# A second place for exponentials, and weight loads on ACT's DMA queue, in an attention kernel with a feed-forward part

## The chip, the cores and the metric

The kernel runs on one core of a Trainium2 chip. The core's engines work side by side, each through its own list of instructions in order: PE (TensorE: matmuls and transpositions, with PEld for loading its stationary operand), DVE (VectorE), ACT (ScalarE), POOL (GpSimd), and SP (SyncE), which here issues DMAs. Engines wait for each other by semaphores. Data lies in HBM, in SBUF (128 partitions) or in PSUM, where PE writes. The metric is the time of one execution in microseconds (us) on the device; less is better.

## What is computed

Softmax attention over 8 batches x 8 heads x 576 rows of width 64, in which each row keeps only the scores within tau of its maximum, and then a feed-forward layer on the 4608 tokens (512 wide, 2048 hidden, softplus between):

```python
scores = scale * np.matmul(q, k.transpose(0, 1, 3, 2))
thresh = np.max(scores, axis=-1, keepdims=True) - tau
scores = np.where(scores >= thresh, scores, -1000000000.0)
scores = scores - np.max(scores, axis=-1, keepdims=True)
attn = np.exp(scores)
attn = attn / (np.sum(attn, axis=-1, keepdims=True) + 1e-09)
attn_out = np.matmul(attn, v).astype(np.float32)
x = np.ascontiguousarray(attn_out.transpose(0, 2, 1, 3)).reshape(B * S, H * D)
h = x @ w_in
g = np.maximum(h, 0.0) + np.log1p(np.exp(-np.abs(h)))
return (g @ w_out).astype(np.float32)
```

`w_in` and `w_out` come as 64-bit floats; the kernel reads them as pairs of 32-bit words and makes 32-bit floats of them on the chip.

## The kernel before

**Attention.** A unit is one pair of heads of one batch: 32 units, nine tiles each, 288 tiles in all. A tile is 128 query rows against 576 keys. Tiles 0 to 3 belong to the unit's first head, tiles 5 to 8 to its second, and tile 4 (`NC`) holds the last 64 rows of both. `mate` makes pairs of tiles 0 and 1, 2 and 3, 5 and 6, 7 and 8; tile 4 is alone.

For each tile, PE makes the scores in one of two PSUM banks (`scores`, L423). DVE takes the row's maximum and a threshold (`row_max`, L430 and L431). ACT takes the exponentials of all scores into SBUF, into one half of `e_all` (`exps`, L435). DVE multiplies them by "score at or above threshold" in place and sums them (`mask`, L440). PE transposes the result (`weights_T`, L474, four blocks of 128 columns; L471 and L477 for the last 64), ACT copies it out (`weights_hi`, L498 to L515), and PE multiplies it with the values (`values`; in the first units by `slow_products`, L549, three matmuls per tile).

`e_all` has two halves of 576 columns. Tiles use them by turns (`half`, the parity of the tile's number in the whole order). The two tiles of a pair lie so that their last 64 columns are neighbours; for the second tile of a pair, L471 transposes 128 columns that run across the border of the halves, for both tiles at once.

In the first five units (`NF`, attribute `whole`, 45 tiles) the weights stay in one 32-bit part and the products are fp32. From the sixth unit on they are split in a high and a low part, and the low part goes to buffers of tag `gL` (two of them). For the first 36 tiles (`TG`) the transposed weights go to PSUM banks of their own; later they go to the bank of the tile's scores.

**Feed-forward.** The tokens go in chunks of 512. For each chunk, x is read back from HBM (`load_x`, L613), split in two parts (`split_x`: L127 on ACT, L132 on POOL), multiplied with `w_in` (`hidden`, L645 to L649), put through softplus (L667) and multiplied with `w_out` (`project`, L703 to L707). The first chunk may start at tile 41. Before it, x of the fourth unit has to be scaled and stored: row scales to HBM (L583), back as `R` (L587), the product on POOL (L593), x out (L597), x in (L613).

**Weights.** There are 32 blocks of 128 x 512 (16 of `w_in`, 16 of `w_out`). `to_f32` loads a block's words (L185, 512 KB), and some steps later ACT takes an absolute value of the high words (L193), POOL clamps it (L194), DVE assembles the bits in three instructions (`second`: L200, L202, L205), and POOL splits the result (L125, L132). `w_in` goes back to HBM in this form (L234) and is read from there in every chunk (L629). `took` is the number of spare buffers that a block got; with two it takes them from the 16 that will hold `w_out`. Block n is begun at tile 2n. `later_(WD, first)` puts the first use four points behind the load; a tile has two points.

**Order.** The program text lists a tile's steps by the letters of `PAT0` (first 36 tiles) or `PAT`. A scheduler then orders the instructions of each engine by its own estimate of times; `behind(i, others)` adds a constraint that instruction i stands after the last of `others` and adds no wait. All DMAs of the kernel before are issued by SP in order; a DMA whose buffer is not free holds those behind it. Every DMA also takes one of eight completion semaphores in turn, and waits until the transfer that used that semaphore before it is complete, wherever that one was issued.

Of the kernel before, what the change touches and what calls it, by code (L numbers as in the profile page):

```python
# [9 lines left out]
F32 = mybir.dt.float32  # L10
F32R = mybir.dt.float32r
U32 = mybir.dt.uint32
AF = mybir.ActivationFunctionType
# [10 lines left out]
P = 128  # L24
# [35 lines left out]
def tile_kernel(ctx: ExitStack, tc: tile.TileContext, q, k, v, tau, w_in, w_out, out):  # L60
# [8 lines left out]
    nc = tc.nc  # L69
    B, H, S, D = q.shape  # L70
    NT, DM = out.shape
    DFF = w_in.shape[1]
    SM = 512
    SR = S - SM
    HS = S // 2
# [60 lines left out]
    free, held = [NFC], [0]  # L136

    masked = []
    scored = []

    def behind(i, others):

        if others:
            tc.add_manual_dep(i.ins, others[-1].ins.name, mybir.DependencyInfo(
                mybir.DependencyClass.NoSync, mybir.DependencyReason.DATA), reason="order")
# [4 lines left out]
    def to_f32(src, want, name, then):  # L150

        keep = 1 if want else 0
        while free[0] < 1 + keep and free[0] < NFC - held[0]:
            force()
        took = max(0, min(2, free[0] - keep))
        if took:
            words = piece(F32R, f"wc_{name}")
        else:  # L160
            words = wpool.tile([P, 2, DM], F32R, tag="wi", bufs=WB, name=f"wc_{name}")
        if took > 1:
            m = piece(F32, f"wa_{name}")[:, 0, :]
        else:
            m = fpool.tile([P, 512], F32, tag="st", bufs=NST, name=f"ws_{name}")
        free[0] -= took + keep
        held[0] += keep

        later_ = defer if took > 1 else lambda n, f: f()
        step = 2 if held[0] < NFC // 2 else 1  # L170
        w = piece(F32R, f"wo_{name}") if want else words

        def done():
            free[0] += took

        def parts():
            hi_of(nc.gpsimd, w[:, 0, :], m)
            lo_of(nc.gpsimd, w[:, 1, :], m, w[:, 0, :])

        if src.dtype == F32:  # L180
            nc.sync.dma_start(m, src)
            later_(WD, lambda: then(parts, w, done))
            return
        words = words.bitcast(U32).rearrange("p a n -> p (a n)")
        nc.sync.dma_start(words, src.bitcast(U32))  # L185
        words = words.rearrange("p (n t) -> p n t", t=2)
        low, high = words[:, :, 0], words[:, :, 1]
        mu = m.bitcast(U32)

        def first():
            nc.scalar.activation(m, high.bitcast(F32), AF.Abs, scale=2.0 ** 16)  # L193
            nc.gpsimd.tensor_scalar(out=m, in0=m, scalar1=W_MAX, scalar2=W_MIN, op0=ALU.min, op1=ALU.max)  # L194
            later_(1, lambda: second(0))


        def second(n):
            if n == 0:
                i = nc.vector.tensor_scalar(out=mu, in0=mu, scalar1=3, scalar2=None, op0=ALU.logical_shift_left)  # L200
            elif n == 1:
                i = nc.vector.scalar_tensor_tensor(out=mu, in0=high, scalar=0x80000000, in1=mu,  # L202
                                                   op0=ALU.bitwise_and, op1=ALU.bitwise_or)
            else:
                i = nc.vector.scalar_tensor_tensor(out=mu, in0=low, scalar=29, in1=mu,  # L205
                                                   op0=ALU.logical_shift_right, op1=ALU.bitwise_or)
            if took > 1:
                behind(i, masked)
            if n < 2:
                later_(step, lambda: second(n + 1))  # L210
            else:
                later_(1, lambda: then(parts, w, done))

        later_(WD, first)
# [184 lines left out]

    e_all = cpool.tile([P, 2, S], F32, name="e_all")
    banks = [ps_s.tile([P, 2, 512], F32, tag="s", name=f"s_{i}") for i in range(SB)]
    nth = [0]

    def scores(s, t):
        if t == s.tiles[0]:
            s.sums = apool.tile([P, 9], F32, tag="sums", name=f"sums_{s.i}")
            s.half, s.sp, s.m, s.grp = {}, {}, {}, {}
        sp = banks[nth[0] % SB]  # L410
        s.half[t] = half = nth[0] % 2
        nth[0] += 1
        s.sp[t] = sp
        if t == NC:
            parts = [(qm[:, n, j, :], j) for j in range(2) for n in range(2)]
        else:
            j = 0 if t < NC else 1
            c = t if t < NC else t - NC - 1
            parts = [(s.qT[j][n][:, c * P:(c + 1) * P], j) for n in range(2)]
        k0 = (1 - half) * SR  # L420
        for m, (lhs, j) in enumerate(parts):
            for hf in range(2):
                i = nc.tensor.matmul(sp[:, hf, 0:HS], lhs, s.kT[j][:, k0 + hf * HS:k0 + (hf + 1) * HS],  # L423
                                     start=(m == 0), stop=(m == len(parts) - 1))
        scored.append(i)
# [6 lines left out]
        s.m[t] = (negm, thr)  # L432

    def exps(s, t):
        nc.scalar.activation(e_all[:, s.half[t], :].rearrange("p (h n) -> p h n", h=2), s.sp[t][:, :, 0:HS],  # L435
                             AF.Exp, bias=s.m[t][0], scale=1.0)

    def mask(s, t):
        e2 = e_all[:, s.half[t], :].rearrange("p (h n) -> p h n", h=2)
        masked.append(nc.vector.scalar_tensor_tensor(  # L440
            out=e2, in0=s.sp[t][:, :, 0:HS], scalar=s.m.pop(t)[1], in1=e2, op0=ALU.is_ge, op1=ALU.mult,
            accum_out=s.sums[:, s.tiles.index(t):s.tiles.index(t) + 1]))
# [8 lines left out]
    def mate(s, t):  # L451

        if t == NC:
            return None, False
        u = t if t < NC else t - 1
        return (t + 1, False) if u % 2 == 0 else (t - 1, True)

    def weights_T(s, t):
        half = s.half[t]
        e = e_all[:, half, :]  # L460
        other, second = mate(s, t)
        lone = other is None
        if 9 * NPAIR * s.b + 9 * s.hp + t < TG:
            main = ps_g.tile([P, NC, P], F32, tag="g", name=f"tm_{s.i}_{t}")
            rest = ps_g.tile([P, NC, P], F32, tag="g", name=f"tr_{s.i}_{t}")[:, 0, :] if lone or second else None
        else:
            sp = s.sp[t]
            main = sp[:, 0, :].rearrange("p (c n) -> p c n", n=P)
            rest = sp[:, 1, 0:P]
        if second:  # L470
            nc.tensor.transpose(rest, e_all.rearrange("p h n -> p (h n)")[:, SM:SM + P], ident)  # L471
        for c in range(NC):
            c0 = half * SR + c * P
            nc.tensor.matmul(main[:, c, :], e[:, c0:c0 + P], ident, is_transpose=True, start=True, stop=True)  # L474
        if lone:
            r0 = 0 if half else SM
            nc.tensor.transpose(rest[0:SR, :], e[:, r0:r0 + SR], ident)  # L477
        s.sp[t] = (main, rest)
# [520 lines left out]
```

## Time and profile before

| what | us |
|---|---|
| time, median of 3 runs (lowest to highest) | 1449.85 (1448.56 to 1451.9) |
| the profiled execution | 1451.43 |
| its span from first to last instruction | 1449.6 |
| PE in the chain of work that ended last | 78% of the span |
| DVE, ACT, DMA and POOL in that chain | 8%, 4%, 3%, 3% |

The profile is of one execution. "Busy" is the time in which an engine had an instruction in work. For an engine that works in order, the idle time ahead of an instruction is put down to what released it last. A row "A <- B: 6.7, 9, 1.7" says that A's engine sat idle ahead of A until B ended, 6.7 us in total, in 9 cases, at most 1.7 us. A row of the timeline gives start, duration, engine, line, operation, and out <- in; in square brackets stands the idle time ahead of it with its releaser. SPq is SP's sequencer, which issues DMAs.

### The profile page before, as it was taken

The page shows a single profiled execution, that of the slowest core. Times are in us where ns is not written, and L with a number is a line of the kernel's source. Part 1 is how long each engine was busy: PE and PEld are TensorE (multiplying, and loading weights), DVE is VectorE, ACT ScalarE, POOL GpSimd, SP SyncE. Part 2 cuts the span into 40 slices and gives each one's busy share as a digit, 9 for nine tenths or more (in the row PEclk, how much of TensorE's full clock was granted, in tenths as well). Part 3 has the DMA queues.
Part 4 walks back from the last instruction along what each step waited for, and adds up shares of the span by engine and source line. Part 5 has one row for each costly group of instructions (what it writes and reads, how often), then busy time and mean ns, then how long its engine had stood idle before and what let it go on. Part 6 is the DMA issues. An engine that isn't in the chain of part 4 may idle for free.

```text
span 1449.6 us, 23487 instructions
## 1 busy us (share of the span) xinstructions
PE 1398.8 (96%) x7860; PEld 1161.8 (80%) x7860; DVE 987.2 (68%) x2211; ACT 847.1 (58%) x1615; POOL 590.3 (41%) x619
## 2 busy tenths in 40 slices
PE   6887999999999999999999999999999999999998
PEld 4555688788888888888888888888888888788886
DVE  6988588787777777777777777777777777402111
ACT  6667667667656576657665665667665765311010
POOL 3667566443333333344334333344334431324221
PEclk9999999999999999999999999999999999999999
DMA  5866765445333533445433533354344432333321
GB/s 170 227 186 206 214 191 182 126 121 160 104 106 114 135 109 116 119 132 151 122 111 96 154 105 100 117 151 120 113 119 135 147 99 73 105 126 130 118 86 44
DMA packets 131208, 189.93 MB, mean 131 GB/s; under 512 B 35312, under 2 KB 86800, under 8 KB 131088
## 3 DMA queue, kind: packets, MB, share of 16 engines
q1 hardware_dynamic: 131088, 188.43, 44.5%
q8 instruction: 63, 1.03, 0.3%
q14 instruction: 57, 0.47, 0.1%
HBM read 140.51 MB, written 27.41 MB: 116 GB/s over the span
## 4 chain that ended last, share of the span: by engine, by line
PE 78%; DVE 8%; ACT 4%; issue 3%; DMA 3%; POOL 3%; SPq 1%; POOLq 0%; DVEq 0%; ACTq 0%
PE s L423 10%; PE h L647 9%; PE h L645 9%; PE h L649 8%; PE o L707 8%; PE o L705 8%; PE o L703 8%; PE s L474 7%; PE pv L555 3%; PE pv L556 3%; PE tr L364 2%; DVE e_all L440 2%; DVE negm L430 2%; POOL g L132 1%; DMA wc_i<-in_moe_w_in_dram 1%
## 5 line engine op out<-in xcount | busy, mean ns | idle before, releaser
L132 POOL TENSOR_TENSOR g<-st,g 128x512 fp32r<-128x512 f32 x144 | 191.6, 1348 | 195.6 <-DVE g L129 184.2
L440 DVE SCALAR_TENSOR_TENSOR e_all<-s,thr,e_all 128x576 f32<-128x576 f32 x288 | 234.6, 816 | 49.1 <-ACT e_all L435 45.8
L430 DVE TENSOR_REDUCE negm<-s 128x1 f32<-128x576 f32 x288 | 217.2, 754 | 43.5 <-PE s L423 36.0
L707 PE MATMUL o<-wo_o,g 128*128 128x512 f32 x576 | 232.5, 404 | 5.3 <-POOL g L132 5.3
L435 ACT ACTIVATE e_all<-s,negm 128x576 f32<-128x576 f32 x288 | 216.0, 750 | 33.5 <-PE tr L471 14.8
L647 PE MATMUL h<-xl,wi 128*128 128x512 f32 x576 | 233.9, 406 | 0.9 <-POOL xl L132 0.9
L703 PE MATMUL o<-wo_o,g 128*128 128x512 f32 x576 | 232.3, 403 | 0.8 <-DVE acc L720 0.4
L645 PE MATMUL h<-xh,wi 128*128 128x512 f32 x576 | 230.6, 400 | 2.3 <-ACT xh L127 2.0
L649 PE MATMUL h<-xh,wi 128*128 128x512 f32 x576 | 230.6, 400 | 0.0
L705 PE MATMUL o<-wo_o,g 128*128 128x512 f32 x576 | 228.4, 397 | 0.0
L498 ACT CAST gH<-s 128x512 fp32r<-128x512 f32 (+1 forms) x270 | 145.1, 550 | 140.6 <-PE s L474 137.8
L132 DVE TENSOR_TENSOR gL<-s,gH 128x512 fp32r<-128x512 f32 (+1 forms) x270 | 169.0, 634 | 46.4 <-ACT gH L498 24.0
L423 PE MATMUL s<-kT,qT 128*128 128x288 f32 x1024 | 193.1, 310 | 7.6 <-ACT gH L512 2.0
L423 PEld LDWEIGHTS s<-kT,qT 128*128 128x128 f32 x1024 | 149.3, 191 | 28.2 <-issue 10.8
L129 DVE CAST g<-st 128x512 fp32r<-128x512 f32 x128 | 57.4, 485 | 149.5 <-ACT st L667 149.0
L474 PE MATMUL s<-identr,e_all 128*128 128x128 f32 x1008 | 154.6, 276 | 3.9 <-DVE e_all L440 3.9
L667 ACT ACTIVATE st<-h 128x512 f32<-128x512 f32 x144 | 78.3, 596 | 115.6 <-PE h L649 115.0
L707 PEld LDWEIGHTS o<-wo_o,g 128*128 128x128 f32 x576 | 108.4, 188 | 29.2 <-POOL g L132 11.0
L474 PEld LDWEIGHTS s<-identr,e_all 128*128 128x128 f32 x1008 | 114.8, 141 | 20.7 <-DVE e_all L440 12.5
L645 PEld LDWEIGHTS h<-xh,wi 128*128 128x128 f32 x576 | 108.9, 189 | 26.1 <-ACT xh L127 2.6
L647 PEld LDWEIGHTS h<-xl,wi 128*128 128x128 f32 x576 | 108.9, 189 | 23.2 <-POOL xl L132 1.7
L649 PEld LDWEIGHTS h<-xh,wi 128*128 128x128 f32 x576 | 109.0, 189 | 21.9
(107 smaller groups left out, 2363.4 us busy)
## 6 DMA issues: line engine op xcount, KB each, us to landing
wi<-wi_d SPq DMA_DIRECT2D x144, 512.0 KB
qT<-qT SPq DMA_DIRECT2D x124, 128.0 KB
R<-r_d SPq DMA_DIRECT2D x64, 144.0 KB
kn<-in_k_dram SPq DMA_DIRECT2D x32, 256.0 KB
qn<-in_q_dram SPq DMA_DIRECT2D x32, 256.0 KB
vn<-in_v_dram SPq DMA_DIRECT2D x32, 256.0 KB
wc_i<-in_moe_w_in_dram SPq DMA_DIRECT2D x16, 512.0 KB
wi_d<-wc_i SPq DMA_DIRECT2D x32, 256.0 KB
```

Of the source, the lines that this page charges most:

```text
L132: eng.tensor_tensor(out=out_, in0=in_, in1=hi.bitcast(F32), op=ALU.subtract)
L423: i = nc.tensor.matmul(sp[:, hf, 0:HS], lhs, s.kT[j][:, k0 + hf * HS:k0 + (hf + 1) * HS], start=(m == 0), stop=(m == len(parts) - 1))
L430: nc.vector.reduce_max(negm, s.sp[t][:, :, 0:HS], axis=AX.XY, negate=True)
L435: nc.scalar.activation(e_all[:, s.half[t], :].rearrange("p (h n) -> p h n", h=2), s.sp[t][:, :, 0:HS], AF.Exp, bias=s.m[t][0], scale=1.0)
L440: masked.append(nc.vector.scalar_tensor_tensor(out=e2, in0=s.sp[t][:, :, 0:HS], scalar=s.m.pop(t)[1], in1=e2, op0=ALU.is_ge, op1=ALU.mult, ...
L474: nc.tensor.matmul(main[:, c, :], e[:, c0:c0 + P], ident, is_transpose=True, start=True, stop=True)
L645: nc.tensor.matmul(h, wi[:, 0, cc, :], u.h[cc], start=(cc == 0), stop=False)
L647: nc.tensor.matmul(h, wi[:, 0, cc, :], u.l[cc], start=False, stop=False)
L649: nc.tensor.matmul(h, wi[:, 1, cc, :], u.h[cc], start=False, stop=(cc == NCC - 1))
L703: nc.tensor.matmul(o, gh[:, sl], wo[fc][:, 0, :], start=(i == 0), stop=False)
L705: nc.tensor.matmul(o, gh[:, sl], wo[fc][:, 1, :], start=False, stop=False)
L707: nc.tensor.matmul(o, gl[:, sl], wo[fc][:, 0, :], start=False, stop=(i == QF - 1))
```

## The change

Exponentials of the first five units go by turns to two places: `e_all` as before, or `e_more`, which takes one of the two buffers of tag `gL`. `pairs` counts pairs and lone tiles (five per unit); both tiles of a pair go to the same place, since L471 reads across their halves, and the next pair to the other. From the sixth unit on there is `e_all` alone. The halves keep their parity.

The load of a weight block with two spare buffers is issued by ACT instead of SP, and is placed behind the exponential that was written last before it. Of 32 loads, 29 go to ACT.

```diff
@@ -182,7 +183,11 @@ to_f32
-        nc.sync.dma_start(words, src.bitcast(U32))
+
+        if took > 1:
+            behind(nc.scalar.dma_start(words, src.bitcast(U32)), powers)
+        else:
+            nc.sync.dma_start(words, src.bitcast(U32))
@@ -399,16 +404,22 @@
     e_all = cpool.tile([P, 2, S], F32, name="e_all")
+    e_more = apool.tile([P, NC, 320], F32R, tag="gL", name="e_more").bitcast(F32)
+    e_more = e_more.rearrange("p c n -> p (c n)")[:, 0:2 * S].rearrange("p (h n) -> p h n", h=2)
+    pairs = [0]
...
     def scores(s, t):
...
         s.half[t] = half = nth[0] % 2
+        pairs[0] += not mate(s, t)[1]
+        s.e[t] = e_more if s.whole and pairs[0] % 2 else e_all
@@ -432,11 +443,11 @@
     def exps(s, t):
-        nc.scalar.activation(e_all[:, s.half[t], :].rearrange("p (h n) -> p h n", h=2), s.sp[t][:, :, 0:HS],
-                             AF.Exp, bias=s.m[t][0], scale=1.0)
+        powers.append(nc.scalar.activation(s.e[t][:, s.half[t], :].rearrange("p (h n) -> p h n", h=2), s.sp[t][:, :, 0:HS],
+                             AF.Exp, bias=s.m[t][0], scale=1.0))
 
     def mask(s, t):
-        e2 = e_all[:, s.half[t], :].rearrange("p (h n) -> p h n", h=2)
+        e2 = s.e[t][:, s.half[t], :].rearrange("p (h n) -> p h n", h=2)
@@ -457,7 +468,7 @@
     def weights_T(s, t):
         half = s.half[t]
-        e = e_all[:, half, :]
+        e = s.e[t][:, half, :]
@@ -468,7 +479,7 @@
-            nc.tensor.transpose(rest, e_all.rearrange("p h n -> p (h n)")[:, SM:SM + P], ident)
+            nc.tensor.transpose(rest, s.e[t].rearrange("p h n -> p (h n)")[:, SM:SM + P], ident)
```

The scheduler makes another order of this. The lines of the changed kernel are up to 11 higher: exponential L446 (before L435), mask L451 (L440), maximum L441 (L430), load L188 (L185), first use of a block L198 (L193). The numbers behind `negm`, `thr`, `tm` and `tr` are tiles of a unit; the last number is a buffer's.

On ACT, at the border of the first and the second unit, there stands before:

```order
L435 ACTIVATE e_all<-s_143,negm_0_494 128x576
L498 COPY gH_3_485<-tm_8_499 128x4x128
L512 ACTIVATE gH_3_485<-tr_8_500,side 128x128 x2
L390 CAST kT_1_447<-tr_1_2_519 128x2x64
L551 COPY xp_302<-pv_2_489 64x320
L435 ACTIVATE e_all<-s_142,negm_1_544 128x576
L498 COPY gH_0_559<-tm_0_549 128x4x128
L193 ACTIVATE wa_i_1_598<-wc_i_1_597 128x512
L435 ACTIVATE e_all<-s_143,negm_2_568 128x576
```

and now:

```order
L446 ACTIVATE e_all<-s_144,negm_0_495 128x576
L198 ACTIVATE wa_i_3_459<-wc_i_3_458 128x512
L523 ACTIVATE gH_3_486<-tr_8_501,side 128x128
L509 COPY gH_3_486<-tm_8_500 128x4x128
L523 ACTIVATE gH_3_486<-tr_8_501,side 128x128
L188 DMA wc_i_0_536<-in_moe_w_in_dram 128x1024
L395 CAST kT_1_448<-tr_1_2_520 128x2x64
L562 COPY xp_303<-pv_2_490 64x320
L446 ACTIVATE e_all<-s_143,negm_1_545 128x576
L509 COPY gH_0_560<-tm_0_550 128x4x128
L446 ACTIVATE e_more<-s_144,negm_2_569 128x576
L198 ACTIVATE wa_i_0_537<-wc_i_0_536 128x512
```

The load of block `i_0` of the second group is now among ACT's instructions, two exponentials ahead of its first use; at the same place in the program the weights are two blocks behind where they were (`wa_i_0` after the exponential of tile 2, before it was `wa_i_1` ahead of it).

On DVE, in tiles 7 and 8 of the first unit, there stands before (`negm` maximum, `thr` threshold, L440 mask, `wa` the weight chain):

```order
L431 TENSOR_SCALAR thr_7_421<-negm_7_420,ntau 128x1
L205 SCALAR_TENSOR_TENSOR wa_i_1_308<-wc_i_1_307,wa_i_1_308 128x512
L200 TENSOR_SCALAR wa_i_2_382<-wa_i_2_382 128x512
L440 SCALAR_TENSOR_TENSOR e_all,sums_218<-s_143,thr_7_421,e_all 128x576
L430 TENSOR_REDUCE negm_8_469<-s_142 128x1
L202 SCALAR_TENSOR_TENSOR wa_i_2_382<-wc_i_2_381,wa_i_2_382 128x512
L431 TENSOR_SCALAR thr_8_470<-negm_8_469,ntau 128x1
L440 SCALAR_TENSOR_TENSOR e_all,sums_218<-s_142,thr_8_470,e_all 128x576
L430 TENSOR_REDUCE negm_0_494<-s_143 128x1
```

and now:

```order
L451 SCALAR_TENSOR_TENSOR e_more,sums_219<-s_144,thr_7_422,e_more 128x576
L441 TENSOR_REDUCE negm_8_470<-s_143 128x1
L205 TENSOR_SCALAR wa_i_2_383<-wa_i_2_383 128x512
L442 TENSOR_SCALAR thr_8_471<-negm_8_470,ntau 128x1
L207 SCALAR_TENSOR_TENSOR wa_i_2_383<-wc_i_2_382,wa_i_2_383 128x512
L441 TENSOR_REDUCE negm_0_495<-s_144 128x1
L442 TENSOR_SCALAR thr_0_496<-negm_0_495,ntau 128x1
L451 SCALAR_TENSOR_TENSOR e_more,sums_219<-s_143,thr_8_471,e_more 128x576
```

The maximum of the next tile now stands ahead of the mask of this one at every second tile.

On SP, from the fourth unit's row scales (`r_d_112`) to the last piece of x for the first chunk (`xst_3`), there stands before:

```order
L583 DMA r_d_112<-rt_1618 9x128
L185 DMA wc_o_1652<-in_moe_w_out_dram 128x1024
L613 DMA xst_1_1719<-x_d_94 128x512
L587 DMA R_1621<-r_d_112 64x576 x2
L613 DMA xst_2_1723<-x_d_94 128x512
L629 DMA wi_0_1733<-wi_d_90 128x1024
L597 DMA x_d_94<-xp_1310 64x576
L597 DMA x_d_94<-xp_1310 64x512
L597 DMA x_d_94<-xp_1310 64x64
L629 DMA wi_1_1735<-wi_d_90 128x1024
L613 DMA xst_3_1729<-x_d_94 128x512
```

and now:

```order
L594 DMA r_d_112<-rt_1619 9x128
L624 DMA xst_2_1724<-x_d_94 128x512
L598 DMA R_1622<-r_d_112 64x576 x2
L314 DMA qn_1957<-in_q_dram 128x2x256
L311 DMA qn_1957<-in_q_dram 64x64 x2
L608 DMA x_d_94<-xp_1311 64x576
L608 DMA x_d_94<-xp_1311 64x512
L608 DMA x_d_94<-xp_1311 64x64
L624 DMA xst_3_1730<-x_d_94 128x512
```

The weight loads `wc_o` and `wi` between them are gone; `wi_0` to `wi_2` stand earlier, from the second unit on.

3 lines of the change are left out of this document (2 added, 1 removed).

## The prediction

> **What bounds the kernel now.** I read the page first, then busy time by stage, then who waits for whom in the first stage, then single instructions there.
>
> ```profile
> span 1449.6 us, 23487 instructions
> PE 1398.8 (96%) x7860; PEld 1161.8 (80%) x7860; DVE 987.2 (68%) x2211; ACT 847.1 (58%) x1615; POOL 590.3 (41%) x619
> ```
>
> PE is busy for 96% of the span, so 50.8 us are free on it. Where they lie decides what the change can be worth. The next rows give busy time by stage: the stretch, its length, then each engine's busy time (and instructions), granted clock, DMA share, GB/s.
>
> ```profile
> core 0: us, PE busy (x) PEld busy (x) DVE busy (x) ACT busy (x) POOL busy (x), PEclk, DMA share, GB/s
> 0.00:20.00 20.00, 9.41 (x44) 8.33 (x44) 10.26 (x25) 9.08 (x19) 5.19 (x13) 1.00 0.60 167
> 20.00:40.00 20.00, 17.54 (x108) 12.30 (x107) 16.96 (x40) 15.43 (x35) 10.13 (x13) 1.00 0.68 201
> 40.00:80.00 40.00, 35.60 (x210) 24.18 (x209) 37.22 (x74) 28.09 (x66) 27.31 (x31) 1.00 0.79 222
> 80.00:120.00 40.00, 32.82 (x187) 22.26 (x186) 31.57 (x68) 27.27 (x66) 26.70 (x31) 0.96 0.59 168
> 120.00:155.00 35.00, 27.32 (x141) 17.29 (x142) 29.43 (x53) 22.18 (x49) 26.51 (x31) 0.98 0.76 226
> ...
> 155.00:1449.60 1294.60, 1276.11 (x7177) 1077.38 (x7175) 861.81 (x1954) 745.01 (x1384) 494.47 (x501) 1.00 0.42 123
> ```
>
> From 155 us on PE is busy for 1276.1 of 1294.6 us: that stage, where the feed-forward matmuls fill every gap, is PE's. Before it PE is idle for 32 us, and in 40 to 80 us DVE is at 37.2 of 40. So the first 155 us are bound by a chain of small steps, with DVE as the most loaded engine, and they hold attention tiles 0 to 43, one exponential each:
>
> ```profile
> L435 ACT ACTIVATE e_all<-s,negm x44: 721/744/782, 12.8 to 153.7; 128x576 f32<-128x576 f32 x44
> ```
>
> The change acts there (45 tiles, and 20 of its 29 moved loads before tile 41). What the first stage loses or gains moves the PE-bound rest as a whole, hence goes one to one into the time.
>
> Next, what DVE waits for there (us in total, times, longest): the first four rows from 20 to 125 us, the last from 125 to 155 us.
>
> ```profile
> DVE e_all L440 <- ACT e_all L435: 6.7, 9, 1.7
> DVE wa_i L200 <- POOL wa_i L194: 4.4, 4, 1.8
> DVE wa_o L200 <- POOL wa_o L194: 2.0, 2, 1.2
> DVE negm L430 <- PE s L423: 1.2, 2, 1.0
> ...
> DVE e_all L440 <- ACT e_all L435: 5.2, 8, 1.3
> ```
>
> The mask (L440) waits 6.7 us for exponentials, and the weight chain (L200 behind POOL's L194) costs 6.4 us. What the exponentials wait for, from 20 to 155 us:
>
> ```profile
> ACT e_all L435 <- PE tr L471: 14.8, 10, 2.9
> ACT wa_i L193 <- DMA wc_i<-in_moe_w_in_dram: 7.1, 5, 3.4
> ACT e_all L435 <- DVE negm L430: 5.4, 7, 1.4
> ACT xh L127 <- DMA xst<-x_d: 2.7, 1, 2.7
> ```
>
> **Part 1, the second place for exponentials.** With one place, the exponential of tile t+1 overwrites a half that the "rest" transposition of tile t (L471) reads, t being the second of a pair. So it waits for mask, then PE, then that transposition: 14.8 us in 10 cases. With places by turns this wait goes. What is late next is seen in one case (start, duration, engine, line):
>
> ```profile
> 85.52 0.81 DVE L440 SCALAR_TENSOR_TENSOR e_all<-s,thr,e_all 128x576 f32<-128x576 f32 x1
> 86.38 2.90 PE L549 MATMUL pv<-gH,vn 128*64 128x320 f32 x6
> 86.48 0.76 DVE L430 TENSOR_REDUCE negm<-s 128x1 f32<-128x576 f32 x1
> ...
> 89.21 0.33 PE L471 MATMUL tr<-identr,e_all 128*128 128x128 f32 x1
> 89.37 0.60 PE L474 MATMUL tm<-identr,e_all 128*128 128x128 f32 x4
> 89.57 0.74 ACT L435 ACTIVATE e_all<-s,negm 128x576 f32<-128x576 f32 x1 [2.89 <-PE tr L471]
> 89.73 0.77 PE L423 MATMUL s<-kT,qT 128*128 128x288 f32 x4
> ...
> 90.35 0.82 DVE L440 SCALAR_TENSOR_TENSOR e_all<-s,thr,e_all 128x576 f32<-128x576 f32 x1 [0.77 <-ACT e_all L435]
> 91.09 0.75 DVE L430 TENSOR_REDUCE negm<-s 128x1 f32<-128x576 f32 x1
> ```
>
> The maximum at 86.48 is ready by 87.24, so the exponential could run there and its mask near 88.1 instead of 90.35, 2.2 us earlier. But the next maximum (91.09) needs scores that PE issues behind the transpositions: they end at 89.73 + 0.77 = 90.50. So the chain gains 91.09 - 90.50 = 0.6 us, not 2.9. Ten waits at 0.5 us give **-5 us**. The bounds are 0 (where DVE was busy anyway, as in 40 to 80 us with 2.8 us free) and 6.7 us, all that DVE lost to exponentials before tile 36. The 5.2 us after 125 us stay: there the order still has maximum, threshold, mask with nothing between that could cover the exponential.
>
> The second place takes one of two buffers of tag gL, which the first five units leave unused. The sixth unit's second group writes that buffer, more than two tiles after the last read of the place. I cost it at nothing; if that cover failed, it would be one wait of the length of a transposition group, 0.6 us.
>
> **Part 2, the weight loads on ACT's queue.** Removed: 29 of the 32 loads from SP's queue, where they stand behind transfers that wait. One case (SP issues; then ACT's first use):
>
> ```profile
> 103.64 0.37 SPq L234 DMA_DIRECT2D wi_d<-wc_i  x1
> 104.06 0.50 SPq L185 DMA_DIRECT2D wc_i<-in_moe_w_in_dram  x1
> ...
> 108.97 0.67 ACT L193 ACTIVATE wa_i<-wc_i 128x512 f32<-128x512 f32 x1 [3.35 <-DMA wc_i<-in_moe_w_in_dram]
> ```
>
> The load stood behind a store that waited for POOL, and ACT, which works in order, then held the next exponential for 3.35 us; the landing took 108.97 - 104.06 = 4.9 us. DVE's 6.4 us of waits for POOL's L194 come from such late blocks. In the new order a load is issued about one and a half tiles ahead of its use, some 4 to 5 us at the pace of 40 to 80 us, which is 40 / 14 = 2.9 us per tile:
>
> ```profile
> L435 ACT ACTIVATE e_all<-s,negm 128x576 f32<-128x576 f32 x14 | 10.5, 749 | 8.2 <-PE tr L471 5.7 <-DVE rs L571 2.4
> ```
>
> That is about a landing. So half the waits may go: **-3 us**, between -6.4 and, where the landing is the longer, +4 (20 loads at 0.2).
>
> On SP's queue the stores, the swaps of qT and the loads of x then stand closer. At the start of the feed-forward part this counts: 2.7 us of ACT's wait above are for the last piece of x.
>
> ```profile
> 144.68 1.77 SPq L597 DMA_DIRECT2D x_d<-xp  x3
> 146.50 0.58 SPq L629 DMA_DIRECT2D wi<-wi_d  x1
> 147.66 0.33 SPq L613 DMA_DIRECT2D xst<-x_d  x1
> ...
> 152.34 0.62 ACT L127 CAST xh<-xst 128x512 fp32r<-128x512 f32 x1 [2.69 <-DMA xst<-x_d]
> ...
> 153.02 0.50 PE L645 MATMUL h<-xh,wi 128*128 128x512 f32 x1 [2.01 <-ACT xh L127]
> ```
>
> That piece took 4.7 us behind a 512 KB weight load. In the new order the weight tiles wi are loaded long before and the piece follows its store directly. Of PE's 2.0 us I take **-1.5** (bounds -2.0 and 0).
>
> Added: each load is an instruction of ACT's. Its issue, where SP did it (min/median/max ns):
>
> ```profile
> L185 SPq DMA_DIRECT2D wc_i<-in_moe_w_in_dram x14: 347/564/1070, 13.5 to 156.9; - x14
> L185 SPq DMA_DIRECT2D wc_o<-in_moe_w_out_dram x8: 364/521/538, 54.9 to 134.3; - x8
> ```
>
> Twenty at 0.55 us are 11 us of ACT before the feed-forward part. ACT is idle for 135 - 93 = 42 us of the 135 from 20 to 155 us (sum of its four rows), and most loads stand behind copies with slack, so I charge a quarter: **+3** (bounds 0 and 11). The trace has no DMA on ACT, so the duration is SP's, the nearest row.
>
> The Trainium skill ("Perfetto Trace Analysis", section "DMA Instruction — HWDGE (DVE, Sync)") says that the issuing sequencer is taken from the end of the wait until the descriptors are made, and only then free for its next instruction. SP's median of 0.56 us agrees for SP; by that rule, if no work of ACT's datapath ran meanwhile, all 11 us would count and the sum below would be 3 us slower instead of 5 faster. No run so far shows it on ACT.
>
> The load also waits: for its buffer, and for one of eight completion semaphores that it shares with earlier transfers on SP's queue. Behind the waiting load stand copies of transposed weights and the next exponential; DVE's mask and PE's next transposition wait for those. Six of the twenty wait for a store (of weights, row scales or x) that itself needs POOL. I charge 0.25 us for each of the six, **+1.5** (bounds 0 and 12, at 2 us each). The nine later loads fall in PE's stage, where feed-forward matmuls cover ACT; I cost them at nothing, and up to 3 us each if softplus is held long enough to starve the projections.
>
> **Sum.** -5 - 3 - 1.5 + 3 + 1.5 = -5.0 us. The profiled execution took 1451.43 us around its span of 1449.6 (1.8 us outside it), so it would take 1446.4. It lay 1.6 us above the median of the runs (1449.85); against that median the forecast is 1444.9, say **1445**.
>
> **Rivals.**
> *PE's order holds the pair.* From 40 to 80 us DVE had only 2.8 us free, and PE's in-order run of transpositions, scores and three slow products per tile may set the pace by itself. Part 1 then gives 1 us and x its 1.5, the loads land no sooner, and issues and waits cost 2 to 4.5: between 0.5 us faster and 2 us slower, 1450. For it: the case above, where 2.9 us of wait are worth 0.6. Against it: DVE is idle for 8.4 of 40 us from 80 to 120.
>
> The Trainium skill ("DMA: Bandwidth & Descriptors", section "Issuing engines are not separate DMA queues") says that transfers from all issuing engines share the same 16 DMA engines, and a second issuer saves only issue time. By it the -3 would be 0 and the sum -2, 1447.9, inside this rival; the case at 104 us speaks against it, since there the order of SP's queue, not the DMA engines, held the load.
>
> *ACT is held by its loads.* One in-order load costs issue plus waiting. The gains are 9.5 us, so with more than 9.5 / 20 = 0.48 us uncovered per load nothing is left, and above 0.62 the kernel is measurably slower; at 0.75 it loses 15 - 9.5 = 5.5 us: 1455. For it: issue alone is 0.55. Against it: ACT's 42 idle us.
>
> *DVE closes up.* If masks always find their exponential and blocks land in time, 6.7 + 6.4 + 1.5 us go against 2 us of cost, 12.6 in all: 1437. Against it: it needs DVE near 100% in all stages.
>
> That the change doesn't do what it says is little likely: the built order shows exponentials in both places and the loads on ACT.
>
> **How the numbers follow.** Forecast (1441 to 1447) 0.38; PE's order, within about 3 us of before, 0.27; ACT held 0.21; DVE closes up 0.14. A measurement of this kernel can tell some 0.2%, 2.9 us, from no change. Faster is 0.38 + 0.14 = 0.52, same 0.27, slower 0.21. The range takes in both outer cases' centres but not their tails: 1437 to 1455.
>
> **What would show it.** Right: the wait of exponentials for L471 falls from 14.8 us to near nothing up to tile 36; DVE's idle time between 20 and 125 us falls by half; the first feed-forward matmuls start about 5 us earlier; PE's busy share after that is unchanged. Wrong: new waits on ACT's queue before exponentials or copies, of DMA issues or of L193 for its block; DVE idle as before but now behind PE's scores; new PE gaps after 155 us, which the first-stage argument doesn't contain. The forecast would fail most simply if the later order, which the scheduler rebuilt up to about the tenth unit, opens gaps there.

## The result, and the profile after

The changed kernel takes **1473.5 us** (median of 6 runs, 1472.4 to 1477.8) against 1450.4 (1448.6 to 1452.5) for the kernel before in the same session: a ratio of 1.0163, 95% interval 1.0147 to 1.018. It is 23 us slower. The forecast was 1445, its range ended at 1455.

The first rows are the totals of the changed kernel, then busy time by stage, with the columns as in the prediction.

```profile
span 1471.2 us, 23476 instructions
PE 1404.4 (95%) x7860; PEld 1166.0 (79%) x7860; DVE 986.5 (67%) x2211; ACT 850.2 (58%) x1615; POOL 589.4 (40%) x619
...
20.00:40.00 20.00, 16.84 (x96) 12.44 (x94) 15.55 (x33) 14.52 (x33) 9.43 (x12) 1.00 0.45 121
40.00:80.00 40.00, 30.23 (x150) 19.40 (x150) 27.14 (x59) 22.37 (x49) 20.05 (x25) 0.88 0.78 225
80.00:120.00 40.00, 31.50 (x180) 22.04 (x179) 31.98 (x64) 26.30 (x58) 22.55 (x27) 0.95 0.63 185
120.00:155.00 35.00, 27.99 (x152) 17.88 (x151) 27.62 (x57) 24.31 (x55) 23.02 (x29) 0.95 0.67 191
155.00:177.00 22.00, 15.16 (x73) 9.94 (x73) 13.60 (x24) 9.26 (x22) 14.67 (x17) 0.84 0.57 169
177.00:1471.20 1294.20, 1274.01 (x7177) 1076.63 (x7176) 860.49 (x1954) 745.13 (x1383) 495.08 (x500) 1.00 0.42 122
```

The last row is the one to compare first. The last 7177 matmuls take 1294.2 us here and took 1294.6 us before. Here they begin at 177 us, before at 155. So PE's stage is untouched, and all of the loss, 22 us of span, lies in the first stage. More than half of it arises by the end of the second unit (12.9 us, table further down): from 40 to 80 us PE ran 150 matmuls against 210 before, and DVE was busy for 27.1 us against 37.2.

What DVE waited for from 20 to 125 us, and four of ACT's waits from 20 to 155 us (total, times, longest):

```profile
DVE negm L441 <- PE s L434: 16.0, 12, 4.8
DVE wa_i L205 <- POOL wa_i L199: 5.1, 2, 4.7
DVE wa_o L205 <- POOL wa_o L199: 2.9, 2, 1.6
DVE e_more L451 <- ACT e_more L446: 0.6, 1, 0.6
...
ACT gH L509 <- PE tm L485: 14.0, 14, 2.8
ACT e_all L446 <- DVE negm L441: 11.7, 10, 4.6
ACT e_more L446 <- DVE negm L441: 5.1, 6, 2.1
...
ACT wa_i L198 <- DMA wc_i<-in_moe_w_in_dram: 0.6, 2, 0.3
```

(Lines of the changed kernel are 11 higher from L430 on: the maximum is L441, exponential L446, mask L451; the weight chain is L198, L199, L205, L207, L210; the row scaling on POOL is L604.) What the change meant to remove is gone: no exponential waits for a transposition, 14.8 us before; masks wait 0.6 us for exponentials, 6.7 before; and ACT waits 0.6 us for weight blocks, 9.1 before. But maxima now wait 16.0 us for PE's scores, 1.2 before, exponentials 16.8 us for maxima, 5.4 before, and DVE still waits 8.0 us for POOL in the weight chain, 6.4 before. ACT's longest wait is new: its copies of transposed weights (L509) wait 14.0 us for PE.

**Where the time goes, first place.** SP's queue at the end of the first unit, two rows of ACT, and PE's matmul that waits:

```profile
34.25 0.37 SPq L314 DMA_DIRECT2D kn<-in_k_dram  x1
34.68 1.12 SPq L311 DMA_DIRECT2D kn<-in_k_dram  x2
...
37.38 0.33 ACTq L188 DMA_DIRECT2D wc_i<-in_moe_w_in_dram  x1
37.75 0.59 ACT L373 CAST kT<-tr 128x512 fp32r<-128x512 f32 x1 [1.05 <-DMA kn<-in_k_dram]
38.45 1.20 SPq L239 DMA_DIRECT2D wi_d<-wc_i  x2
39.76 0.62 SPq L390 DMA_DIRECT2D qT<-qT  x1
40.44 0.86 SPq L391 DMA_DIRECT2D qT<-qT  x1
...
43.28 0.82 PE L434 MATMUL s<-kT,qT 128*128 128x288 f32 x2 [4.12 <-DMA qT<-qT]
```

The swap of qT (two DMAs that copy its halves crosswise), which the next unit's first scores need, stands behind a load of K for a later unit and two stores of weights, and PE stands still for 4.1 us. The load of K is what is new: before, it was issued at 42.41, after the swap, while two stores (at 34.40) stood ahead of the last swap there too. Here it first waited 1.2 us for POOL to be done with its buffer. ACT's load of a weight block then came out only at 37.38, and ACT was idle for 1.05 us ahead of the cast, which the profile puts down to the transfer of K. Only behind that cast did ACT write the last piece of qT. It was ready 2.9 us later than before, and its swap left 0.8 us behind it, 0.2 before.

**Second place.** The row factors of the first unit go to HBM and back (`r_d`, then `R`). SP in the changed kernel:

```profile
56.73 0.49 SPq L594 DMA_DIRECT2D r_d<-rt  x1
57.27 1.30 SPq L326 DMA_DIRECT2D vn<-in_v_dram  x2
59.08 0.37 SPq L640 DMA_DIRECT2D wi<-wi_d  x1
59.70 1.33 SPq L598 DMA_DIRECT2D R<-r_d  x2
```

A load of V and a 512 KB weight tile of the feed-forward part, which is used 100 us later, go ahead of `R`. That alone does not hold its issue: `R` starts 3.0 us behind `r_d`, and before it was 3.4 us, with the load of a weight block between them as well (48.15). But from the end of its issue to the start of POOL's scaling it takes 6.6 us, 4.0 in the kernel q1 below; from 62 to 68 us the DMA engines are busy throughout (share 0.99 and 1.07 in the two halves; 0.69 and 0.80 in q1 from 49 to 55). What follows on POOL, DVE and PE:

```profile
67.62 1.42 POOL L604 TENSOR_TENSOR xp<-xp,R 128x576 f32<-128x576 f32 x1 [3.86 <-DMA R<-r_d]
...
71.07 0.61 POOL L199 TENSOR_SCALAR wa_i<-wa_i 128x512 f32<-128x512 f32 x1
...
71.71 0.43 DVE L205 TENSOR_SCALAR wa_i<-wa_i 128x512 uint32<-128x512 uint32 x1 [4.71 <-POOL wa_i L199]
...
73.58 0.80 DVE L451 SCALAR_TENSOR_TENSOR e_all<-s,thr,e_all 128x576 f32<-128x576 f32 x1
...
74.45 0.61 PE L434 MATMUL s<-kT,qT 128*128 128x288 f32 x1 [4.13 <-DVE e_all L451]
```

POOL works in order. It stood at the row scaling for 3.9 us, so its clamp of a weight block came late; DVE, in order too, stood at that block for 4.7 us with a mask behind it; and PE waited 4.1 us for that mask. Before, the scaling of this unit ran at 55.72 with no wait. Of these 11.9 us, 7.7 were lost ahead of the second place: the row factors themselves came at 54.1 us, 46.4 before.

### The profile page after: what moved, and what is told of

Same layout as the page of the kernel before. It is cut to its first block, busy times and chain, and to the rows that moved or that the text cites. A ratio compares the mean times of both kernels' runs of the same rounds, so it can differ in the third digit from the quotient of the medians.

```text
span 1471.2 us, 23476 instructions
## 1 busy us (share of the span) xinstructions
PE 1404.4 (95%) x7860; PEld 1166.0 (79%) x7860; DVE 986.5 (67%) x2211; ACT 850.2 (58%) x1615; POOL 589.4 (40%) x619
## 4 chain that ended last, share of the span: by engine, by line
PE 79%; DVE 6%; ACT 4%; POOL 3%; issue 3%; DMA 3%; SPq 1%; POOLq 0%; ACTq 0%
PE s L434 11%; PE h L658 9%; PE h L656 8%; PE h L660 8%; PE o L718 8%; PE o L716 7%; PE o L714 7%; PE s L485 7%; PE pv L567 3%; PE pv L566 3%; PE tr L369 2%; PE pv L560 2%; DVE negm L441 1%; ACT L678 1%; POOL g L132 1%
## 5 line engine op out<-in xcount | busy, mean ns | idle before, releaser
L441 DVE TENSOR_REDUCE negm<-s 128x1 f32<-128x576 f32 x288 | 217.2, 754 | 60.3 <-PE s L434 52.5
L451 DVE SCALAR_TENSOR_TENSOR e_all<-s,thr,e_all 128x576 f32<-128x576 f32 x265 | 215.7, 815 | 41.6 <-ACT e_all L446 38.7
L509 ACT CAST gH<-s 128x512 fp32r<-128x512 f32 (+1 forms) x270 | 145.0, 550 | 140.5 <-PE s L485 137.2
L446 ACT ACTIVATE e_all<-s,negm 128x576 f32<-128x576 f32 x265 | 199.0, 751 | 21.8 <-DVE negm L441 19.7
L485 PE MATMUL s<-identr,e_all 128*128 128x128 f32 x988 | 151.3, 275 | 5.2 <-DVE e_all L451 5.1
L656 PEld LDWEIGHTS h<-xh,wi 128*128 128x128 f32 x576 | 108.4, 188 | 29.2 <-ACT xh L127 5.5
L718 PEld LDWEIGHTS o<-wo_o,g 128*128 128x128 f32 x576 | 108.4, 188 | 29.1 <-POOL g L132 10.9
L714 PEld LDWEIGHTS o<-wo_o,g 128*128 128x128 f32 x576 | 108.5, 188 | 23.3 <-ACT acc L729 1.9
```

The lines of the kernel that those rows point to most:

```text
L441: nc.vector.reduce_max(negm, s.sp[t][:, :, 0:HS], axis=AX.XY, negate=True)
L446: powers.append(nc.scalar.activation(s.e[t][:, s.half[t], :].rearrange("p (h n) -> p h n", h=2), s.sp[t][:, :, 0:HS], AF.Exp, bias=s.m[t][ ...
L451: masked.append(nc.vector.scalar_tensor_tensor(out=e2, in0=s.sp[t][:, :, 0:HS], scalar=s.m.pop(t)[1], in1=e2, op0=ALU.is_ge, op1=ALU.mult, ...
L656: nc.tensor.matmul(h, wi[:, 0, cc, :], u.h[cc], start=(cc == 0), stop=False)
L714: nc.tensor.matmul(o, gh[:, sl], wo[fc][:, 0, :], start=(i == 0), stop=False)
L718: nc.tensor.matmul(o, gl[:, sl], wo[fc][:, 0, :], start=False, stop=(i == QF - 1))
```

## Experiments

### Which part of the change

Four kernels, each with one part left out or altered.

```diff
 # p1_place: the second place alone
+        nc.sync.dma_start(words, src.bitcast(U32))
 # p2_loads: the loads alone
+        s.e[t] = e_all
 # p3_both_free: both, no order behind the exponentials
+            nc.scalar.dma_start(words, src.bitcast(U32))
 # p4_both_sp: both, but issued by SP
+            behind(nc.sync.dma_start(words, src.bitcast(U32)), powers)
```

> Second place for exponentials alone; all weight loads back on SP's queue. Three theories for the 23 us that the whole change costs. LATE (loads held behind exponentials make the scheduler start the weight blocks later): this kernel has no such loads, so 1443 to 1450. QUEUE (a load standing in ACT's or out of SP's queue costs): the same, 1443 to 1450. PLACE (the second place makes the scheduler order maxima and scores badly, DVE then waits for scores): 1465 to 1475, with DVE's wait of maxima for scores near the 17.0 us of the changed kernel (1.2 before).

> Loads on ACT's queue behind exponentials alone; one place for exponentials. LATE and QUEUE: 1465 to 1475, with waits of POOL's row scaling for R as in the changed kernel. PLACE: 1446 to 1455, since the second place is gone.

> Second place and loads on ACT's queue, but without the order behind the exponentials: the first blocks are prepared after 0 to 12 exponentials again, against 3 to 18 in the changed kernel and 2 to 15 before. LATE: 1443 to 1452. QUEUE and PLACE: 1465 to 1475.

> Second place, and the loads ordered behind the same exponentials but issued on SP's queue, so that the first blocks come as late as in the changed kernel (after 3 to 18 exponentials). LATE: 1463 to 1478, as slow as the changed kernel. QUEUE: 1443 to 1452. PLACE: 1465 to 1475.

| kernel | us | ratio to before (95%) |
|---|---|---|
| p1_place | 1455.1 | 1.0023 (1.0011 to 1.0034) |
| p2_loads | 1469.8 | 1.0129 (1.0107 to 1.015) |
| p3_both_free | 1468.9 | 1.0115 (1.0092 to 1.0139) |
| p4_both_sp | 1458.8 | 1.0041 (1.0026 to 1.0056) |

The kernels with loads on ACT's queue are slow, the others nearly are not. LATE falls with p3 and p4, PLACE with p1 and p2. QUEUE has the right sign in all four, though p1 and p4 lie 5 and 7 us above the ranges that it gave. And it can mean two things. A scheduler orders each engine's list by its own estimate, and with the loads on ACT it built other lists: in tiles 0 to 44, the changed kernel has 22 masks behind the maximum of the next tile, p4 has 8 and the kernel before 11.

### The queue itself, or the order that is built for it

At the end of the kernel's text each engine's instructions were tied, one behind the other, in the order taken from another kernel; the weight loads on ACT's queue were left out of that. Such a tie adds no wait; two kernels that are tied in the order of the kernel before (q4 and, below, v3) run in its time.

```diff
+    for e, steps_ in _json.loads(_zlib.decompress(_b64.b85decode(ORDER))).items():
...
+            if i is None or i.name in loads_:
+                continue
+            if prev is not None:
+                tc.add_manual_dep(i, prev.name, mybir.DependencyInfo(
+                    mybir.DependencyClass.NoSync, mybir.DependencyReason.DATA), reason="order")
```

> Second place, loads on ACT's queue behind exponentials as in the changed kernel, but every engine's instructions (loads apart) are held in the order that the fourth kernel had, the one with the same loads on SP's queue (1458.8 us). ORDER (the scheduler builds another order when the loads stand on ACT's queue, and that order costs the time): 1455 to 1463. MACHINE (a load issued by ACT itself costs the time, by holding ACT or by running beside SP's transfers): 1468 to 1478, as the changed kernel.

> The reverse: the order of the changed kernel on every engine, but the loads issued on SP's queue behind the same exponentials. ORDER: 1467 to 1478. MACHINE: 1455 to 1463.

> One place for exponentials, the order of the kernel before on every engine, and only the loads moved to ACT's queue, each as soon as its buffer is free. This is the move of the loads by itself. ORDER: 1445 to 1454; by my prediction's terms (-3 for loads that land earlier, -1.5 for x, +3 for issue, +1.5 for waits) no change against before. MACHINE: 1462 to 1472.

> The second place by itself, with the order of the kernel before on every engine. My prediction gave it -5 us (between 0 and -6.7), so 1445 to 1451 against 1451.7 if its mechanism is right and only the rebuilt order hid it. If the pair is held by the order of PE and DVE in any case (the rival), 1450 to 1453.

| kernel | order of | loads on | us | ratio to before (95%) |
|---|---|---|---|---|
| q1_order4_act | p4 | ACT | 1455.4 | 1.0032 (1.0020 to 1.0045) |
| q2_orderafter_sp | changed | SP | 1468.9 | 1.0117 (1.0104 to 1.013) |
| q3_orderbefore_act | before | ACT | 1463.6 | 1.0087 (1.0072 to 1.0103) |
| q4_orderbefore_place | before | SP | 1450.9 | 1.0000 (0.9989 to 1.0012) |

The order decides most. The same loads on the same queue, within one exponential of the same places, take 1.63% over before in the one order and 0.32% in the other: **1.31%, 19 us, is the price of the order alone** with the loads on ACT's queue. On SP's queue the same step costs less, 0.76% or 11 us (q2 against p4). With p4's order the queue makes no difference that can be told (1.0032 on ACT, 1.0041 on SP). In the changed kernel's order it does: 1.0163 on ACT, 1.0117 on SP, 6.7 us, for which no run gives the cause. They are lost by the second unit (row factors at 87.5 against 80.9 us, table below).

q3 came out in the range of MACHINE, 1462 to 1472, and against ORDER: here the queue costs 12.6 us with the order held. Its loads were left free, and two things show in its trace. The first 512 KB block goes out ahead of the first K, so that the first exponential starts at 16.1 us, 12.8 before. And ACT reaches a load only in its turn, often just ahead of the use: ACT waits 13.6 us for blocks of `w_in` from 20 to 155 us, 7.1 before. These make 9.8 of the 12.6 us, if both go into the time in full, which no run shows. In the changed kernel, where the loads stood behind exponentials and well ahead of their use, ACT waited 0.6 us. So what the queue costs depends on the order and on the place of the loads in it: nothing in p4's order, 6.7 us in the changed kernel's, 12.6 here.

q4 is the second place by itself in the order of the kernel before, and it is worth nothing there. Its waits (ACT 20 to 155 us, DVE 20 to 125 us):

```profile
ACT wa_i L244 <- DMA wc_i<-in_moe_w_in_dram: 10.0, 5, 3.6
ACT e_more L492 <- DVE negm L487: 6.2, 7, 2.0
ACT e_all L492 <- DVE negm L487: 5.7, 5, 2.7
...
DVE wa_i L251 <- POOL wa_i L245: 7.7, 4, 3.0
DVE e_more L497 <- ACT e_more L492: 3.5, 3, 2.5
DVE wa_o L251 <- POOL wa_o L245: 1.6, 2, 1.2
DVE e_all L497 <- ACT e_all L492: 1.2, 3, 0.5
DVE negm L487 <- PE s L480: 1.0, 1, 1.0
```

The 14.8 us for transpositions are gone, but exponentials now wait 11.9 us for their maxima (5.4 before), and ACT 10.0 us for blocks (7.1 before). DVE stands still for 15.0 us in these rows; in the kernel before the same rows gave 6.7 + 4.4 + 2.0 + 1.2 = 14.3. The wait was passed on, and DVE got nothing of it.

### Which engine's order

The changed kernel with its own order held, edited on some engines. v1 moves 16 masks ahead of the next maximum; v2 takes POOL's and SP's lists from p4; v4 does both; v3 takes the kernel before and moves 12 masks behind the next maximum.

> The changed kernel with its own order held on every engine, except that at 16 tiles from 8 to 36, where DVE's mask of a tile stands behind the maximum of the next tile (in the order of the 1458.8 us kernel it does not), the mask is put ahead of that maximum. MASK (a mask behind the next maximum makes PE's transposition of this tile wait for the next tile's scores, which PE computes ahead of it): 1456 to 1466, and DVE's wait of maxima for scores between 20 and 160 us falls from 17.0 to under 8 us. POOL (POOL's row scaling, which waits 9.2 us for its factors, holds the weight blocks, and these DVE): 1470 to 1476. REST (the order of PE or ACT): 1470 to 1476.

> The changed kernel with its own order held on PE, DVE and ACT, but POOL's and SP's instructions in the order of the 1458.8 us kernel. POOL: 1462 to 1469, and the waits of row scaling for its factors fall from 9.2 to under 3 us. MASK and REST: 1470 to 1476.

> Both edits together: masks ahead of the next maximum, POOL and SP in the other order. MASK with POOL explain the order's loss if this comes to 1453 to 1460, as the kernel with that order on all engines (1455.4); if it stays above 1464, PE's or ACT's order holds a third part.

> The kernel before, its own order held on every engine, except that at 12 tiles (8, 12, 14, 16, 18, 20, 22, 24, 26, 32, 34, 36) the mask is put behind the next tile's maximum, as the changed kernel has it. MASK: slower by 4 to 12 us, 1455 to 1463. POOL and REST: 1449 to 1453, no change.

| kernel | us | ratio to before (95%) |
|---|---|---|
| v1_maskfirst | 1469.3 | 1.0121 (1.0088 to 1.0154) |
| v2_poolsp | 1479.9 | 1.0189 (1.0160 to 1.0218) |
| v4_mask_poolsp | 1472.7 | 1.0149 (1.0123 to 1.0175) |
| v3_before_masklast | 1450.7 | 1.0002 (0.9988 to 1.0016) |

The masks are worth some 6 us of the 19, less than expected (the intervals of v1 and the changed kernel just overlap), and v3 shows that a mask behind the next maximum costs nothing by itself. That it costs where the maximum waits for scores that are late for another reason is likely, and not shown by a run of its own. v2 was slower, against every expectation, although POOL's waits for `R` were gone as its expectation had it. Its trace shows a reason: p4's list brings the pieces of x later than ACT's list of the changed kernel casts them, and ACT waits 21.6 us for them at the start of the feed-forward part, 9.0 us in the changed kernel. So lists of two kernels can't be mixed where one engine's list leans on another's. The next four took p4's lists only up to the first piece of x: SP's (w0), SP's and POOL's (w1), then also the masks (w2) and PE's two differing places (w3).

> The changed kernel with its own order held on every engine, but SP's transfers up to the first piece of x in the order of the 1458.8 us kernel (the weight tiles of the feed-forward part are not loaded yet there, and the row factors' trip and the swaps of qT go ahead of the loads of later units). SP (512 KB weight tiles and later units' loads, which the scheduler drew forward into the emptied queue, hold the row factors and the swaps): 1461 to 1468, and POOL's wait for the row factors falls from 9.2 to under 4 us. MASK or ACT/PE: 1470 to 1476.

> As w0, and POOL's work up to the first piece of x in that order too. SP: about the time of w0, within 3 us. POOL (row scaling and weight blocks stand badly to each other): at least 4 us below w0. In v2 the same two orders had brought the ends of the first three units 5.7, 8.7 and 10.7 us forward, so 1460 to 1466 if nothing is given back.

> As w1, with the 16 masks ahead of the next maximum on DVE. If the two add (6 us for the masks as measured in v1), 1454 to 1461; if they share the same waits, within 2 us of w1.

> As w2, with PE's order changed at the two places where it differs in the first four units (at the ends of units 1 and 3 a score product that waits for the swap of qT stands ahead of the transpositions of the tile before). PE: 2 to 6 us below w2, near the 1455.4 us of the kernel that has the other order on all engines. ACT (its order of copies, exponentials and weight steps): no change against w2, and w2 and w3 stay over 1460.

They took 1495.5, 1479.9, 1474.1 and 1473.5 us (1.0295, 1.0190, 1.0152, 1.0146). w0 to w2 come out above their forecasts; w3 brings no change against w2, as ACT had it. ACT again waits 17 us for x in w1 to w3. In w0, where SP has p4's list and POOL has not, POOL waits 36.8 us from 20 to 155 us, in three cases, for loads of Q that SP brings later than POOL's list asks for them. The masks are worth 5.5 us once more (w1 to w2), PE's two places nothing (0.9 us, intervals overlap). The stage by itself can be read from another row, ACT's copy of a unit's row factors (`rt`), which comes once a unit. Its start in us:

| kernel | unit 0 | unit 1 | unit 2 | unit 3 | unit 4 |
|---|---|---|---|---|---|
| before | 46.4 | 74.6 | 103.7 | 133.7 | 181.4 |
| changed | 54.1 | 87.5 | 120.3 | 151.1 | 201.6 |
| q1 (p4's order) | 46.5 | 73.3 | 104.2 | 135.5 | 187.8 |
| q2 (changed order, SP) | 50.3 | 80.9 | 114.5 | 145.1 | 196.5 |
| w0 | 46.8 | 86.8 | 124.0 | 167.9 | 222.9 |
| w1 | 46.4 | 73.8 | 107.2 | 143.4 | 204.5 |
| z2 (below) | 53.8 | 84.4 | 115.4 | 145.8 | 197.9 |

With SP's list of p4 alone, w0 already loses nothing in unit 0, where the changed kernel loses 7.7 us: that part is SP's list. With POOL's list as well, w1 loses nothing in the first two units, where the changed kernel loses 12.9 us; it gives this back from unit 2 on. The last pair is the reverse: q1, into which the changed kernel's lists are put for the first units, SP's and POOL's (z2) or ACT's (z1).

> Loads on ACT's queue and the order of the 1458.8 us kernel on every engine, as in the kernel that measured 1455.4, except that SP's and POOL's work up to the stores of unit 1's x stands in the order of the changed kernel: SP loads weight tiles and pieces for the feed-forward part and the inputs of units 3 and 5 there, ahead of the row factors and swaps. SP AND POOL: 8 to 14 us over 1455.4, 1463 to 1470, with unit 1's row factors copied after 82 us (73.3 in that kernel). ACT: within 3 us of 1455.4.

> The same kernel with only ACT's work up to the 28th exponential (three units) in the order of the changed kernel. ACT: 1463 to 1472. SP AND POOL: within 4 us of 1455.4.

z2 takes 1467.9 us, 1.0117 (1.0096 to 1.0138): 0.85% or **12.3 us over q1** from SP's and POOL's lists of the first two units. z1 takes 1457.5 us, 1.0049 (1.0033 to 1.0065), 2.5 us over q1 with intervals that overlap. Both came as SP AND POOL had forecast them. Of the two places above, z2 has the first again, at the swap of qT, where q1 has no wait; at the second, the row scaling of unit 0 does not wait for `R`:

```profile
42.44 0.70 PE L485 MATMUL s<-kT,qT 128*128 128x288 f32 x2 [4.18 <-DMA qT<-qT]
...
66.93 1.41 POOL L655 TENSOR_TENSOR xp<-xp,R 128x576 f32<-128x576 f32 x1
```

So the price of the two lists is shown, and the swap is part of it; how it divides among the single transfers, and between SP and POOL beyond unit 0, is not.

SP of q1 at the first place: no load of K stands there, and the last swap goes ahead of the weight stores.

```profile
35.47 0.46 SPq L580 DMA_DIRECT2D qT<-qT  x1
35.99 0.59 SPq L581 DMA_DIRECT2D qT<-qT  x1
36.68 1.39 SPq L429 DMA_DIRECT2D wi_d<-wc_i  x1
```

Not tried: the list of PE, DVE or ACT alone taken whole from p4 into the changed kernel. No run was faster than the kernel before, and none pointed to one that would be.

## Why the prediction was wrong

**What bounds the kernel: right.** The first stage's loss went one to one into the time, and PE's stage after it is the same (1294.2 and 1294.6 us). So what was costed at nothing there, the second place's buffer and the nine later loads, did cost nothing.

**The step that failed** is in part 2, in the sentence "In the new order the weight tiles wi are loaded long before and the piece follows its store directly", which was booked as **-1.5**, and in the one before it, by which the swaps "then stand closer" on SP's queue. The early tiles were a fact, and it was read with the wrong sign. Those tiles, and later units' K and V, were drawn forward into the queue that the weight loads had left, ahead of the swaps and the row factors, which the chain of small steps waits for. SP's and POOL's lists of the first two units cost 12.3 us (z2 against q1), of which the late swap is seen in both traces. The piece of x came late as well, PE waiting 5.1 us for it, not 2.0:

```profile
171.04 0.79 PE L656 MATMUL h<-xh,wi 128*128 128x512 f32 x1 [5.06 <-ACT xh L127]
```

The prediction named a rebuilt order that opens gaps as the way in which it would fail most simply, but gave it no price and no chance, and expected the gaps after 155 us. Another of its signs did come: DVE idle behind PE's scores. With the masks (5.5 to 6 us, v1 and w2) the sum is near the order's 19 us; these pieces come from different kernels and need not add. The 6.7 us that the queue costs in the changed order stay open.

**Part 1, -5 us: 0.** q4 gives between 1.6 us faster and 1.7 slower. The wait for L471 did go. But the gain of one maximum, 0.6 us, was taken as a gain of the chain ten times over. The worked case itself can be followed in q4: the exponential ran at 87.31 instead of 89.57. Its mask did not follow near 88.1, as the prediction had it, but at 89.58, since DVE's list has the weight block's L200 ahead of it, which waits 1.2 us for POOL in both kernels. The next maximum, at 90.31 instead of 91.09, did gain 0.8 us. Six us later DVE gave it back to the next block (the kernel before, then q4):

```profile
95.75 0.43 DVE L200 TENSOR_SCALAR wa_i<-wa_i 128x512 uint32<-128x512 uint32 x1 [0.26 <-POOL wa_i L194]
96.61 0.82 DVE L440 SCALAR_TENSOR_TENSOR e_all<-s,thr,e_all 128x576 f32<-128x576 f32 x1 [0.43 <-ACT e_all L435]
...
96.22 0.43 DVE L251 TENSOR_SCALAR wa_i<-wa_i 128x512 uint32<-128x512 uint32 x1 [1.54 <-POOL wa_i L245]
96.56 0.81 DVE L497 SCALAR_TENSOR_TENSOR e_all<-s,thr,e_all 128x576 f32<-128x576 f32 x1
```

Over the stage the exponentials wait for maxima instead, and DVE is idle as long as before. The low bound, 0, was the answer. In the order that the scheduler builds for it, the second place costs 3.3 us (p1).

**Part 2, landing, -3 us.** The loads did come in time on ACT's side (0.6 us of waits). DVE's waits for POOL were to fall from 6.4 to half; they rose to 8.0, of which 4.7 are the one case in which POOL was held by its row scaling.

**Part 2, issue +3 and waits +1.5.** In p4's order the move to ACT's queue, with the gain of landing in it, changes nothing that can be told (q1 against p4). Up to 178 us, 21 of the changed kernel's 22 loads on ACT began while ACT's instruction ahead of them was still at work, and one held ACT, for about 1 us (at 37.38). The rival "ACT is held by its loads" forecast a slower kernel at 1455, the right side; such holds make a small part of the loss, but the queue's 6.7 us in the changed order have no known cause, so it is not refuted there.

**The rival "PE's order holds the pair"** came nearest for part 1: it gave 1 us where 0 was measured. That a rebuilt order turns the sign was no rival at all.

## What to carry to other kernels

Where a scheduler builds the order, moving a DMA to another queue is two changes: read the whole new list of the queue that became empty, ask of each transfer that moved forward which small, urgent transfer now stands behind it, and give that a price and a chance. To tell a change from the order that is built around it, tie the engines in a given order and change one thing. A wait that is the last one before an instruction is worth its length only if nothing else would end just before it. Read the list of the engine behind it on to its next wait, and take the bound 0 seriously when that one is of the same size.

## What the runs showed of the hardware

A pause of PE is followed by slower matmuls. Stretches of the changed kernel with the granted clock in the third column from the end, each pause followed by what came after it:

```profile
39.00:43.00 4.00, 0.16 (x2) 0.00 (x0) 0.30 (x1) 1.33 (x3) 1.02 (x1) 0.99 1.01 276
43.00:46.00 3.00, 2.72 (x6) 1.48 (x7) 1.83 (x5) 1.07 (x2) 0.00 (x0) 0.50 0.33 114
...
71.00:74.40 3.40, 0.00 (x0) 0.00 (x0) 2.65 (x6) 1.05 (x3) 2.48 (x3) 0.88 0.57 138
74.40:77.00 2.60, 2.55 (x9) 2.12 (x10) 1.05 (x3) 1.01 (x3) 1.71 (x2) 0.50 1.04 305
77.00:80.00 3.00, 3.00 (x7) 0.98 (x5) 2.42 (x8) 0.92 (x2) 0.81 (x2) 0.50 0.91 232
```

Behind these two pauses of about 4 us the granted clock is 0.50 for 3 and for 5.6 us, and then 0.95 (46 to 49 us) and 0.93 (80 to 83 us). A third, from 100 to 104.7 us, is followed by 0.54 for 3.3 us. The mean clock from 40 to 80 us is 0.88, 1.00 before. So each of the two pauses above is likely to have cost more than its 4.1 us; no run separates the part of the clock from that of the order. In the first 26 us the column shows 1.00 although four scores take 1.31 us there (at 17.69) and 0.77 later (at 27.64), so it does not catch every slow stretch. The Trainium skill ("TensorE: Matmul & The Clock Gate", section "Part 1: The HAM clock gate (the "warmup" mystery)") says that an idle window of about 3.4 us halves the clock and that about as long a busy stretch restores it. The halving agrees; the way back agrees behind the first and the third pause and was longer behind the second.

The issue of a load on ACT takes less than on SP, and it runs while ACT's datapath works. All issues of `w_in` blocks on ACT (min/median/max ns), and one of a `w_out` block beside an activation:

```profile
L188 ACTq DMA_DIRECT2D wc_i<-in_moe_w_in_dram x16: 334/334/402, 14.1 to 198.6; - x16
...
131.65 0.67 ACT L198 ACTIVATE wa_i<-wc_i 128x512 f32<-128x512 f32 x1
131.70 0.34 ACTq L188 DMA_DIRECT2D wc_o<-in_moe_w_out_dram  x1
```

0.33 us against SP's 0.52 to 0.56: twenty issues are 6.7 us and not 11. The second issue began while the activation ahead of it in ACT's list was still at work. The rule on the issuing sequencer ("Perfetto Trace Analysis" of the Trainium skill, section "DMA Instruction — HWDGE (DVE, Sync)") says that it is free only when the descriptors are made. The prediction drew a loss of 11 us from it for the case that no work of ACT's datapath runs meanwhile. That condition does not hold here: in 21 of 22 loads the sequencer is taken while the datapath works.
